# Corner scores of the next heads placed behind the corner of the value sums, ScalarE's other work held back around the sigmoids, and three buffers for v

## The chip, the cores and the metric

The kernel runs on one core of one Trainium2 chip. The metric is the device time of one execution in microseconds (us). Engines: TensorE (PE), VectorE (DVE), ScalarE (ACT), GpSimd (POOL), and SyncE (SP), whose queue issues nearly all DMAs.

## The reference

For 4 batches of 12 heads with 448 positions and head size 64, sigmoid attention; its output goes through a channel mix and then a mixer with a Fourier transform and a feed-forward network:

```python
scores = scale * np.matmul(q, k.transpose(0, 1, 3, 2)) - np.log(S)
attn = 1.0 / (1.0 + np.exp(-scores))
x = np.matmul(attn, v)                      # heads side by side: 768 columns
xk = mu_k * x + (1.0 - mu_k) * x_prev       # x_prev: the position before
k = np.maximum(xk @ w_k, 0.0)
v = k * k @ w_v
r = 1.0 / (1.0 + np.exp(-(xr @ w_r)))       # xr: the same mix with mu_r
# then real(fft2(r*v)) added, a norm, two matmuls with w_ch1 and w_ch2, a sum
```

All is kept near float32: where a product runs in the faster fp32r form, each operand is split into a high and a low part, and three products (high-high, high-low, low-high) are summed.

## The kernel before

The change lies in the first stage, which computes attention and, between its pieces, the keys (`xk @ w_k`). A *pair* is two heads on the 128 partitions: 24 pairs, numbered 0 to 23, six per batch. Pairs go in rounds of two; "round 8" is pairs 8 and 9. A round issues on TensorE, in `attention()`, `both()` and `attnv()`:

- `attnv(i-2)`: the value sums of the two pairs of the round before: first the *corner* of both (tiles `av` from `sg_c`, the last 64 positions), then the rest (`av_6`, `av_7`: 24 matmuls from `sg` and `v`). `join` then copies each sum from PSUM to SBUF on ScalarE (`x<-av`), which frees its PSUM tile, stores `x`, and mixes it (`mix_k`, `xkh`, `xkl`).
- `corner(i)`: the corner scores of the two new pairs (`sc_c`), each head's last 64 positions, from the raw `k` and `q`.
- `scores(i)`, later `scores(i+1)`: six score tiles each (`sc`). `weigh` turns each tile into weights with a sigmoid on ScalarE (`sg<-sc`). Pairs 0 to 5 use float32 matmuls, later ones three fp32r products of split `k` and `q`; the split is a cast on ScalarE (`kh`, `qh`) and a subtraction on VectorE (`kl`, `ql`).

Score tiles, corner tiles and (from pair 6 on) the sums `av` share six PSUM tiles, taken in turn (`slot`). A round takes 2 for `av`, 2 for the corner, 6 and 6 for the scores. So scores 3 and 4 of a round's first pair take over the tiles of its two `av`, once `x<-av` has read them.

Between these pieces TensorE gets the matmuls of the keys (`k`, 18 for each of 8 tiles of a batch). Their results use two further PSUM tiles in turn (`bank`). `key_done` has ScalarE apply relu (`kt<-k`, which frees the tile) and square, then cast to the high part (`kp<-kt`); VectorE subtracts, and SP's queue stores both parts (`k2_d<-kp`). `kp` has two buffers, so the cast of a key tile waits until the store of the tile two before has landed. `k`, `q` have two raw buffers each, `v` two.

The order of every queue is set while the program is built: the class `Order` walks generators in a modelled time, and each engine's instructions stand in the order in which the generators emit them. Its model has costs of engines and DMAs and no PSUM or SBUF tile that is still taken; on the chip each engine works in the emitted order and waits on semaphores. `PACES` are due times in a round for the second scores and for the next round; `o.feed` holds key matmuls that fill the gaps; `weights()` splits the weights for the keys and later stages on VectorE (`LATER`: when it begins, `EVERY`: its pace).

Of the kernel before, what the change touches and what calls it, by code (L numbers as in the profile page):

```python
# [12 lines left out]
F32 = mybir.dt.float32  # L13
F32R = mybir.dt.float32r
# [6 lines left out]
B, H, S, DH = 4, 12, 448, 64  # L21
# [9 lines left out]
PACES = (12.6, 19.6)  # L31
BEGIN = 3
HELD = 4
LATER = 8.0
EVERY = (9.6, 8.5)

SL = np.r_[np.arange(2, 129, 2), np.arange(1, 128, 2)]
LL = np.r_[0, np.arange(130, 255, 2), np.arange(129, 256, 2)]
# [79 lines left out]
class Order:  # L118
# [9 lines left out]
    def __init__(self, nc):  # L128
        self.nc = nc
        self.now = 0.0  # L130
        self.free = {}
        self.heap = []
        self.count = 0
        self.hold = False
        self.rate = 340e3
        self.feed = deque()
        self.at = {}
# [17 lines left out]
    def others(self):  # L155

        self.hold = True
        yield self.now

    def run(self, until=None):  # L160

# [95 lines left out]
def build(tc, ap):  # L257
    nc = tc.nc
    V, G = nc.vector, nc.gpsimd
    o = Order(nc)  # L260
# [7 lines left out]
    def shift(pl, name, n=1):  # L268
        pl.tile([128, int(16 * n)], F32, tag=f"shift_{name}", name=f"shift_{name}", bufs=1)
# [83 lines left out]
    att = pool(s_r, "att", 2, "right")  # L353
# [5 lines left out]
    wkh = wkp.tile([128, NF, KD, 128], F32R, name="wkh")  # L359
    wkl = wkp.tile([128, NF, KD, 128], F32R, name="wkl")  # L360

    pair_t, raw_t, sg_t, xk_t = {}, {}, {}, {}
    pairs = [(b, p) for b in range(B) for p in range(NP)]
    WHOLE = NP

    def prepare(what):

        def room_for(i):
            if what == "v":
                return ("av", i - 2) if i > 1 else None  # L370
            if i < WHOLE:
                return ("pair", i - 4) if i > 3 else None
            return ("pair", 2 * i - 10) if i < WHOLE + 2 else (what, i - 2)

        for i, (b, p) in enumerate(pairs):
            if room_for(i):
                yield from o.issued(room_for(i))
            if what != "v" and i > WHOLE + 1:
                yield from o.issued(("corner", (i - 2) // 2 * 2))
            shape = {"k": [128, 4, 128], "q": [128, S], "v": [128, 4, 2, DH]}[what]  # L380
            odd = what != "v" and i < WHOLE and i % 2
            if what == "q" and i == 1:
                shift(att, "qh")
            raw = att.tile(shape, F32, tag=what + "h" if odd else what, name=f"{what}_{i}", bufs=2)
            if i == 0 and what == "k":
                o.dma(raw[:, 0], ap[what][b, p, :, 0])
                t = o.dma(raw[:, 1:4], ap[what][b, p, :, 1:4])
            else:
                if i == 0 and what == "v":
                    nc.scalar.activation(raw[:, 0, 0, 0:1], bias_s, AF.Sigmoid)  # L390
                t = o.dma(raw, ap[what][b, p], nc.scalar if what == "q" and i < 2 else None)
            if what == "v" or i < WHOLE:
                pair_t[what, i] = raw_t[what, i] = raw
                o.at[what, i] = o.at["raw", what, i] = t
                yield o.now if i == 0 and what != "v" else t
            else:
                raw_t[what, i] = raw
                o.at["raw", what, i] = t
                yield t
                yield from o.issued(("pair", 2 * i - 9 if i < WHOLE + 2 else i - 2))  # L400
                if i == WHOLE:
                    shift(att, "att" + what, 1 + (what == "k"))
                hi, lo = (att.tile(shape, F32R, tag=what + x, name=f"{what}{x}_{i}", bufs=2) for x in "hl")
                pair_t[what, i] = hi, lo
                yield o.act(hi, raw)
                o.at[what, i] = t = o.sub(V, lo, raw, hi)
                yield t

    places = [(c, j) for c in range(3) for j in range(2)]
    half = [slice(0, 64), slice(64, 128)]
# [28 lines left out]
    def corner(i):  # L441
        yield from o.need(*(("raw", w, i + m) for m in range(2) for w in "kq"))
        ps = [slot(f"sc_{i}_c{j}") for j in range(2)]
        for j in range(2):
            for m in range(2):
                k, q = raw_t["k", i + m], raw_t["q", i + m]
                o.mm(ps[j][half[m], 0:S], k[half[j], 3, 64 * j : 64 * j + 64], q[half[j]], True, True, 0.21)
        o.at["corner", i] = o.now
        yield from o.others()
        for j in range(2):  # L450
            weigh(i, f"c{j}", ps[j])
        yield from o.others()

    def both(i, t0):
        if i > 0:
            yield from corner(i)
        yield from o.need(("k", i), ("q", i))
        yield from scores(i)
        if i == 0:
            yield from corner(i)  # L460
        o.at["pair", i] = o.now
        if i > WHOLE + 1:
            yield t0 + PACES[0] * (len(o.feed) > 0)
        yield from o.need(("k", i + 1), ("q", i + 1))
        yield from scores(i + 1)
        o.at["pair", i + 1] = o.now

    def attnv(i):
        ps = [(bank if i < WHOLE else slot)(f"av_{i + m}") for m in range(2)]
        yield from o.need(("sg", i, "c0"), ("sg", i, "c1"))  # L470
        for m in range(2):
            v = pair_t["v", i + m]
            for j in range(2):
                o.mm(ps[m][half[j], 0:S], v[half[m], 3, j], sg_t[i, f"c{j}"][half[m]], True, False, 0.21, skip=True)
        yield from o.others()
        for m in range(2):
            v = pair_t["v", i + m]
            for n, (c, j) in enumerate(places):
                yield from o.need(("sg", i + m, n))
                sg = sg_t.pop((i + m, n))  # L480
                o.mm(ps[m][half[j], 0:S], v[:, c, j], sg, False, c == 2, 0.39, skip=True)
                yield from o.others()
            o.at["av", i + m] = o.now
            o.spawn(join(i + m, ps[m]), o.now + 0.2)

    def join(i, ps):
        if i > 1:
            yield from o.issued(("mixed", i - 2))
        x = att.tile([128, S + 1], F32, tag="x", name=f"x_{i}")
        G.memset(x[:, 0:1], 0.0)  # L490
        yield o.act(x[:, 1 : S + 1], ps[:, 0:S])
        b, p = pairs[i]
        o.dma(x_d[b][p], x)
        if b > 1:
            yield from o.issued(("key", b - 2))
        xh = mop.tile([128, S], F32R, tag=f"xkh{p}", name=f"xkh_{i}")
        xl = mop.tile([128, S], F32R, tag=f"xkl{p}", name=f"xkl_{i}")
        xk_t[b, p] = (xh, xl)
        yield from mix(x, mu_k, att, p, f"k{i}", xh, xl, ("xk", b, p))
        o.at["mixed", i] = o.now  # L500

    def mix(x, mu, pl, p, nm, xh, xl, key, bufs=2):
        xk = pl.tile([128, S], F32, tag="mix", name=f"mix_{nm}", bufs=bufs)
        early = nm[0] == "k" and int(nm[1:]) < WHOLE
        if early:
            yield o.ts(xk, x[:, 1 : S + 1], mu[:, 0, p : p + 1], None, ALU.mult, ALU.bypass)
        else:
            yield o.act(xk, x[:, 1 : S + 1], AF.Copy, scale=mu[:, 0, p : p + 1])
        yield o.stt(xk, x[:, 0:S], mu[:, 1, p : p + 1], xk, ALU.mult, ALU.add)
        if early:  # L510
            V.tensor_copy(xh, xk)
            yield o.spend(V, 0.34)
        else:
            yield o.act(xh, xk)
        o.at[key] = t = o.sub(V, xl, xk, xh)
        yield t
# [6 lines left out]
    def attention():  # L523
        for i in range(0, len(pairs) + 2, 2):
            t0 = o.now
            if i > 0:
                yield from o.need(("v", i - 2), ("v", i - 1))
                yield from attnv(i - 2)
            if i < len(pairs):
                yield from both(i, t0)  # L530
            yield t0 + PACES[1] * (len(o.feed) > 0)
        yield from o.need(("xk", B - 1, NP - 1))
        o.at["attention"] = o.now

    def key_done(b, f, ps):
        t = mop.tile([128, S], F32, tag="kt", name=f"kt_{b}_{f}")
        o.act(t, ps, AF.Relu)
        yield o.act(t, t, AF.Square)
        parts = mop.tile([128, 2, S], F32R, tag="kp", name=f"kp_{b}_{f}")
        yield o.act(parts[:, 0], t)  # L540
        yield o.sub(V, parts[:, 1], t, parts[:, 0])
        o.at["k2_d", b, f] = o.dma(k2_d[b][f], parts.bitcast(F32)) + 2.0
        yield o.now
# [21 lines left out]
    for f in range(NF + KD):  # L565
        if f < NF:
            src, hl, key = ap["w_k"][f], [w[:, f].rearrange(flat) for w in (wkh, wkl)], ("wk", f)
# [195 lines left out]
    for i, n in enumerate((113, 112, 112, 111)):  # L763
        c = fp.tile([128, 2, TW], F32R, name=f"ct{i}")
# [862 lines left out]
```

## Time and profile before

| | us |
|---|---|
| Median of 3 runs (lowest, highest) | 1166.37 (1165.54, 1166.45) |
| The profiled execution: its own time | 1166.35 |
| Its span, first to last instruction | 1164.5 |
| PE busy in the span | 1155.5 (99%) |
| ACT busy in the span | 572.6 (49%) |
| Attention and keys, on PE's timeline | 3.9 to 263.9 |

The profile is one execution. Matmuls overlap in it: each runs into the next, and one that waits for a tile is shown as long, not as late. So "busy" on PE includes some waiting, and the distance from one start to the next tells more than the share.

### The profile page before, as it was taken

To read this page: it belongs to the slowest core of one execution; us is meant where nothing else is said; L and a number is where in the kernel's file an instruction comes from. 1 tells how busy PE (TensorE), PEld (TensorE's weight loads), DVE (VectorE), ACT (ScalarE), POOL (GpSimd) and SP (SyncE) were. 2 spreads that over 40 slices of the span, in tenths; PEclk is the share of its full clock that TensorE was granted. 3 is DMA by queue.
4 is the path that set the end of the run, shared out by engine and by line. 5 is a ranking of instruction groups with operands and counts; after the bars stand their busy time and mean duration, and the time that the engine had idled before them with its cause. 6 is when DMAs were issued, how large, how long until landed. Compare 5 with 4: busy or idle time off the path is not lost.

```text
span 1164.5 us, 16614 instructions
## 1 busy us (share of the span) xinstructions
PE 1155.5 (99%) x6094; PEld 1011.3 (87%) x6094; DVE 836.5 (72%) x1381; ACT 572.6 (49%) x1051; POOL 96.4 (8%) x138
## 2 busy tenths in 40 slices
PE   8999999999999999999999999999999999999998
PEld 3666667699999999999999999999999999999998
DVE  4777776655743688899988888786567777777762
ACT  6878787765630132243333333333237566665740
POOL 0000000000000000000000000000003143342420
PEclk9999999999999999999999999999999999999999
DMA  6667688868949456377565656654827696978894
GB/s 242 226 207 250 219 313 337 304 243 267 325 152 293 158 175 213 121 276 288 183 236 187 223 197 205 219 191 179 312 95 158 145 197 103 188 132 179 173 200 162
DMA packets 93926, 246.67 MB, mean 212 GB/s; under 512 B 10706, under 2 KB 46612, under 8 KB 93716
## 3 DMA queue, kind: packets, MB, share of 16 engines
q1 hardware_dynamic: 77764, 217.29, 53.0%
q0 software_dynamic: 15792, 27.86, 15.1%
q8 instruction: 48, 0.79, 0.3%
q10 hardware_dynamic: 288, 0.46, 0.1%
q14 instruction: 34, 0.28, 0.1%
HBM read 147.02 MB, written 100.61 MB: 213 GB/s over the span
## 4 chain that ended last, share of the span: by engine, by line
PE 97%; ACT 1%; DMA 1%; issue 0%; SPq 0%; DVE 0%
PE f L189 32%; PE m L189 11%; PE v L189 10%; PE k L189 10%; PE r L189 7%; PE av L189 6%; PE f_W L189 4%; PE sc L189 4%; PE f_X L189 4%; PE f_Z L189 4%; PE f_Y L189 2%; PE pq L189 1%; PE sc_c L189 1%; PE pa L189 1%; PE qa L189 1%; DMA v<-in_v 1%
## 5 line engine op out<-in xcount | busy, mean ns | idle before, releaser
L189 PE MATMUL f<-un,w1h 128*128 128x448 f32 x576 | 164.0, 364 | 0.0
L189 PE MATMUL f<-h,w2h 128*128 128x448 f32 x576 | 163.2, 363 | 0.0
L248 POOL DMA_DIRECT2D u_d<-stage x75 | 64.9, 938 | 603.1 <-DMA m_d<-stage 531.7
L189 PEld LDWEIGHTS f<-un,w1h 128*128 128x128 f32 x576 | 108.1, 188 | 7.5 <-issue 0.6
L189 PEld LDWEIGHTS f<-h,w2h 128*128 128x128 f32 x576 | 108.2, 188 | 7.0
L224 DVE TENSOR_TENSOR acc<-acc,f 128x448 f32<-128x448 f32 x126 | 76.3, 618 | 50.1 <-PE f L189 49.3
L189 PE MATMUL v<-k,wvh 128*128 128x448 f32 x384 | 111.9, 365 | 0.0
L189 PE MATMUL f<-un,w1l 128*128 128x448 f32 x288 | 103.9, 361 | 0.0
L189 PE MATMUL f<-h,w2l 128*128 128x448 f32 x288 | 103.7, 360 | 0.0
L189 PE MATMUL m<-hs,sw_h 128*128 128x448 f32 x324 | 91.4, 363 | 0.0
L243 ACT ACTIVATE sg<-sc,bias_s 128x448 f32<-128x448 f32 x144 | 79.0, 663 | 4.3 <-PE sc L189 4.3
L232 DVE SCALAR_TENSOR_TENSOR w_bits<-w_raw,w_bits 128x768 uint32<-128x768 uint32 x80 | 76.5, 956 | 1.7
L189 PEld LDWEIGHTS v<-k,wvh 128*128 128x128 f32 x384 | 72.0, 188 | 4.9 <-issue 0.6
L243 ACT ACTIVATE h<-f 128x448 fp32r<-128x448 f32 x48 | 26.2, 546 | 92.7 <-PE f L189 92.7
L189 PE MATMUL k<-xkh,wkh 128*128 128x448 f32 x192 | 70.7, 368 | 0.0
L189 PE MATMUL k<-xkl,wkh 128*128 128x448 f32 x192 | 70.4, 367 | 0.0
L189 PE MATMUL k<-xkh,wkl 128*128 128x448 f32 x192 | 70.0, 365 | 0.0
L189 PE MATMUL v<-k,wvl 128*128 128x448 f32 x192 | 69.7, 363 | 0.0
L189 PEld LDWEIGHTS m<-hs,sw_h 128*128 128x128 f32 x324 | 60.8, 188 | 4.0
L241 ACT COPY stage<-m 128x448 f32<-128x448 f32 x105 | 55.9, 536 | 15.9 <-DMA u_d<-stage 10.4
L189 PE MATMUL m<-hs,sw_l 128*128 128x448 f32 x162 | 58.4, 360 | 0.0
L189 PEld LDWEIGHTS f<-un,w1l 128*128 128x128 f32 x288 | 53.9, 187 | 3.9 <-issue 0.2
(230 smaller groups left out, 2520.2 us busy)
## 6 DMA issues: line engine op xcount, KB each, us to landing
w_raw<-in_w SPq DMA_DIRECT2D x40, 768.0 KB, 4.8
u_d<-stage POOLq DMA_DIRECT2D x75, 224.0 KB, 5.9
w_d<-w_bits SPq DMA_DIRECT2D x40, 384.0 KB, 2.6
k_d<-kp SPq DMA_DIRECT2D x32, 448.0 KB, 4.1
k<-k_d SPq DMA_DIRECT2D x32, 448.0 KB, 6.0
a<-w_d SPq DMA_DIRECT2D x24, 384.0 KB, 5.7
w<-w_d SPq DMA_DIRECT2D x24, 384.0 KB, 10.8
v<-in_v SPq DMA_DIRECT2D x24, 256.0 KB, 3.6
```

What stands on the lines that cost most here:

```text
L189: self.nc.tensor.matmul(out, lhs, rhs, start=start, stop=stop, skip_group_check=skip)
L224: eng.tensor_tensor(out, a, c, op=op)
L232: self.nc.vector.scalar_tensor_tensor(out, a, scalar, c, op0=op0, op1=op1)
L241: self.nc.scalar.copy(out, a)
L243: self.nc.scalar.activation(out, a, fn, **kw)
L248: self.nc.gpsimd.dma_start(out, src, accum_op=ALU.add)
```

## The change

The corner scores of the next two pairs move from behind the value sums to directly behind the corner of the value sums (except rounds 2 and 6, `BEHIND`). In round 2 the second pair's sums come between its two blocks of scores (`TURNS`). `v` gets three buffers. While a round's scores are due or running, `calm()` holds back new work for ScalarE: casts of `k` and `q`, mixes, squares and casts of keys; `soon()` sets that flag, `begin()` and `both()` clear it. Splits of `k` and `q` become generators of their own (`divide`). The weights begin at 13.5 in place of 8.0 and go at 9.0 in place of 9.6.

```diff
-LATER = 8.0
-EVERY = (9.6, 8.5)
+LATER = 13.5
+AHEAD = 1.0
+NV = 3
+TURNS = (2,)
+BEHIND = (2, 6)
+EVERY = (9.0, 8.5)
...
+    def calm(self):
+
+        while self.quiet:
+            yield self.now + 0.1
...
-                return ("av", i - 2) if i > 1 else None
+                return ("av", i - NV) if i >= NV else None
...
-                yield from o.issued(("corner", (i - 2) // 2 * 2))
+                yield from o.issued(("corner", (i - 2) // 2 * 2), (what, i - 2))
...
+    def divide(what, i, raw, shape):
+        yield from o.issued(("pair", 2 * i - 9 if i < WHOLE + 2 else i - 2))
+        if i > WHOLE:
+            yield from o.issued((what, i - 1))
+        yield from o.calm()
...
+        yield o.act(hi, raw)
+        o.at[what, i] = t = o.sub(V, lo, raw, hi)
+        yield t
...
+    def soon(*keys):
+        o.quiet = all(k in o.at for k in keys)
+
+    def both(i, t0, turn=None):
+        if i in BEHIND:
             yield from corner(i)
...
-        if i > WHOLE + 1:
+        o.quiet = o.quiet and i < WHOLE
+        if turn:
+            yield from turn
+        if i >= WHOLE:
+            yield t0 + (PACES[0] - AHEAD) * (len(o.feed) > 0)
+            soon(("k", i + 1), ("q", i + 1))
             yield t0 + PACES[0] * (len(o.feed) > 0)
...
+        o.quiet = False
+
+    def begin(i):
         ps = [(bank if i < WHOLE else slot)(f"av_{i + m}") for m in range(2)]
         yield from o.need(("sg", i, "c0"), ("sg", i, "c1"))
+        o.quiet = False
...
+    def attnv(i):
+        v = pair_t["v", i]
+        for n, (c, j) in enumerate(places):
...
+            if i % 2 and n == 2 and i < len(pairs) - 2 and i + 1 not in TURNS:
+                g = i + 1
+                soon(("k", g), ("q", g))
...
                 yield from o.need(("v", i - 2), ("v", i - 1))
+                yield from begin(i - 2)
+                if i < len(pairs) and i not in BEHIND:
+                    yield from corner(i)
                 yield from attnv(i - 2)
+                turn = attnv(i - 1)
+                if i not in TURNS:
+                    yield from turn
+                    turn = None
             if i < len(pairs):
-                yield from both(i, t0)
+                yield from both(i, t0, turn)
```

`calm()` is also called ahead of the mixes on ScalarE in `mix`, and of the square and the cast in `key_done`. After the stage the orders agree but for single rows that change places.

What this makes of the orders, at three places. TensorE at the start of round 8, before: the last of `av_7`, the corner of pairs 8 and 9, their first scores.

```order
L189 MATMUL av_7_823<-sg_7_4_737,v_7_650 64x448
L189 MATMUL av_7_823<-sg_7_5_739,v_7_650 64x448
L189 MATMUL sc_8_c0_863<-q_8_701,k_8_652 64x448
L189 MATMUL sc_8_c0_863<-q_9_801,k_9_795 64x448
L189 MATMUL sc_8_c1_864<-q_8_701,k_8_652 64x448
L189 MATMUL sc_8_c1_864<-q_9_801,k_9_795 64x448
L189 MATMUL sc_8_0_881<-qh_8_772,kh_8_746 128x448
```

TensorE at the same place in the changed kernel.

```order
L199 MATMUL av_6_764<-sg_6_c0_646,v_6_511 64x448
L199 MATMUL av_6_764<-sg_6_c1_648,v_6_511 64x448
L199 MATMUL av_7_765<-sg_6_c0_646,v_7_604 64x448
L199 MATMUL av_7_765<-sg_6_c1_648,v_7_604 64x448
L199 MATMUL sc_8_c0_777<-q_8_640,k_8_638 64x448
L199 MATMUL sc_8_c0_777<-q_9_660,k_9_658 64x448
L199 MATMUL sc_8_c1_778<-q_8_640,k_8_638 64x448
L199 MATMUL sc_8_c1_778<-q_9_660,k_9_658 64x448
L199 MATMUL av_6_764<-sg_6_0_663,v_6_511 64x448
```

The corner scores now stand between the corner and the rest of the value sums, and the scores follow the sums directly.

ScalarE at the start of round 14, before: `x_12`, `x_13` are the copies of the value sums, `kt` and `kp` belong to keys, `sg_14` are sigmoids.

```order
L241 COPY x_12_1502<-av_12_1476 128x448
L243 ACTIVATE mix_k12_1513<-x_12_1502,mu_k_243 128x448
L241 COPY x_13_1520<-av_13_1477 128x448
L243 ACTIVATE kt_1_0_1527<-k_1_0_1404 128x448
L243 ACTIVATE kt_1_0_1527<-kt_1_0_1527 128x448
L243 ACTIVATE mix_k13_1534<-x_13_1520,mu_k_243 128x448
L241 CAST kh_15_1536<-k_15_1489 128x512
L241 CAST qh_15_1545<-q_15_1492 128x448
L241 CAST xkh_12_1511<-mix_k12_1513 128x448
L241 CAST kp_1_0_1555<-kt_1_0_1527 128x448
L243 ACTIVATE sg_14_c0_1560<-sc_14_c0_1548,bias_s_241 128x448
```

ScalarE at the same place in the changed kernel.

```order
L253 ACTIVATE kt_0_7_1457<-kt_0_7_1457 128x448
L251 CAST kp_0_6_1461<-kt_0_6_1381 128x448
L253 ACTIVATE sg_14_c0_1493<-sc_14_c0_1482,bias_s_241 128x448
L253 ACTIVATE sg_14_c1_1495<-sc_14_c1_1483,bias_s_241 128x448
L251 CAST kp_0_7_1503<-kt_0_7_1457 128x448
L251 COPY x_12_1516<-av_12_1473 128x448
L251 COPY x_13_1546<-av_13_1474 128x448
L253 ACTIVATE sg_14_0_1549<-sc_14_0_1536,bias_s_241 128x448
```

Mixes and casts of `k` and `q` have left the place between the copies and the sigmoids; the cast `kp_0_7` now stands ahead of the copies. It writes the buffer that the store of `kp_0_5` reads.

SP's queue in round 14 of the changed kernel: raw `k` and `q` of the pairs to come, then that store.

```order
L260 DMA wr_2_raw_1447<-in_w_r 128x1536
L260 DMA k_16_1488<-in_k 128x512
L260 DMA q_16_1490<-in_q 128x448
L260 DMA k_17_1498<-in_k 128x512
L260 DMA q_17_1500<-in_q 128x448
L260 DMA k2_d0_5_88<-kp_0_5_1409 128x896
```

In the kernel before, `k2_d0_5` follows a weight load (`wr_0_raw`) that is not tied to a corner; now it follows four loads, the first of which waits until the corner scores of pair 14 have been computed, since they read the buffer.

## Rows read from the trace of the kernel before

**Rows 1.** Page, part 1: engine, busy us, share of the span, instructions.
```profile
PE 1155.5 (99%) x6094; PEld 1011.3 (87%) x6094; DVE 836.5 (72%) x1381; ACT 572.6 (49%) x1051; POOL 96.4 (8%) x138
```

**Rows 2.** Windows: stretch, then PE, PEld, DVE, ACT, POOL busy us (instructions), clock, DMA.
```profile
160.00:180.00 20.00, 20.00 (x121) 13.56 (x119) 9.19 (x15) 15.89 (x30) 0.20 (x2) 1.00 0.83 313
```

**Rows 3.** Chain that ended last: start us, us, work; pieces that run without a wait.
```profile
9.47 2.46 PE sc L189 x12
...
70.94 2.01 PE sc L189 x18
72.96 5.21 PE k L189 x25
...
83.74 0.91 PE sc_c L189 x8
84.65 2.16 PE sc L189 x18
```

**Rows 4.** The same chain: pieces of scores that take longer.
```profile
18.41 5.45 PE sc L189 x23
...
30.34 4.39 PE sc L189 x19
34.76 1.54 PE sc L189 x4
...
43.59 2.15 PE sc L189 x18
...
48.89 8.80 PE k L189 x43
```

**Rows 5.** Timeline of PE: start us, us, instruction [idle before]; heads 10 to 19.
```profile
113.60 0.97 PE L189 MATMUL av<-sg_c,v 64*64 64x448 f32 x4 [0.30 <-ACT sg L243]
...
115.75 4.73 PE L189 MATMUL av<-sg,v 128*64 128x448 f32 x24
...
123.34 0.47 PE L189 MATMUL sc<-qh,kh 64*128 64x448 f32 x2
...
126.86 0.48 PE L189 MATMUL k<-xkh,wkh 128*128 128x448 f32 x1
...
195.46 0.47 PE L189 MATMUL sc<-qh,kh 64*128 64x448 f32 x2
...
198.22 0.47 PE L189 MATMUL k<-xkh,wkl 128*128 128x448 f32 x1
```

**Rows 6.** Timeline of ScalarE (ACT) in one round: start us, us, instruction.
```profile
67.36 0.70 ACT L243 ACTIVATE mix_k<-x,mu_k 128x448 f32<-128x448 f32 x1
67.92 0.59 ACT L241 CAST xkh<-mix_k 128x448 fp32r<-128x448 f32 x1
...
71.96 3.26 ACT L243 ACTIVATE sg<-sc,bias_s 128x448 f32<-128x448 f32 x6
...
75.08 0.60 ACT L241 CAST kp<-kt 128x448 fp32r<-128x448 f32 x1
75.53 0.59 ACT L243 ACTIVATE kt<-k 128x448 f32<-128x448 f32 x1
76.15 0.58 ACT L243 ACTIVATE kt<-kt 128x448 f32<-128x448 f32 x1
76.64 0.60 ACT L241 CAST kh<-k 128x512 fp32r<-128x512 f32 x1
77.15 0.56 ACT L241 CAST qh<-q 128x448 fp32r<-128x448 f32 x1
```

**Rows 7.** Timeline of SP's queue: two loads issued behind each other.
```profile
64.27 0.33 SPq L250 DMA_DIRECT2D k<-in_k  x1
64.66 0.43 SPq L250 DMA_DIRECT2D q<-in_q  x1
```

**Rows 8.** Waits of SP's queue, 40 to 264 us: us in total, times, longest.
```profile
SPq L250 <- PE sc_c L189: 7.0, 6, 2.2
```

**Rows 9.** Tile k_d (a key part's store), 50 to 264 us: issue to landing.
```profile
DMA to landing us min/median/max: 2.4/4.2/7.3
```

More of the change, by code (lines that the diff above doesn't have):

```diff
@@ L134, in __init__ @@
         self.hold = False
+        self.quiet = False
         self.rate = 340e3
@@ L360, in build @@
     wkl = wkp.tile([128, NF, KD, 128], F32R, name="wkl")
-    pair_t, raw_t, sg_t, xk_t = {}, {}, {}, {}
+    pair_t, raw_t, sg_t, xk_t, av_t = {}, {}, {}, {}, {}
     pairs = [(b, p) for b in range(B) for p in range(NP)]
@@ L383, in prepare @@
                 shift(att, "qh")
-            raw = att.tile(shape, F32, tag=what + "h" if odd else what, name=f"{what}_{i}", bufs=2)
+            raw = att.tile(shape, F32, tag=what + "h" if odd else what, name=f"{what}_{i}", bufs=NV if what == "v" else 2)
             if i == 0 and what == "k":
@@ L394, in prepare @@
                 o.at[what, i] = o.at["raw", what, i] = t
-                yield o.now if i == 0 and what != "v" else t
+                yield o.now if (i == 0 and what != "v") or (i > NV and what == "v") else t
             else:
@@ L398, in prepare @@
                 o.at["raw", what, i] = t
[L399 to L407, printed above, removed]
+                o.spawn(divide(what, i, raw, shape), t)
+                yield o.now + 0.2
+    def divide(what, i, raw, shape):
[3 more added lines that the diff above has]
+        yield from o.calm()
+        if i == WHOLE:
+            shift(att, "att" + what, 1 + (what == "k"))
+        hi, lo = (att.tile(shape, F32R, tag=what + x, name=f"{what}{x}_{i}", bufs=2) for x in "hl")
+        pair_t[what, i] = hi, lo
+        yield o.act(hi, raw)
+        o.at[what, i] = t = o.sub(V, lo, raw, hi)
+        yield t
     places = [(c, j) for c in range(3) for j in range(2)]
@@ L452, in corner @@
         yield from o.others()
-    def both(i, t0):
-        if i > 0:
+    def soon(*keys):
+        o.quiet = all(k in o.at for k in keys)
+    def both(i, t0, turn=None):
+        if i in BEHIND:
             yield from corner(i)
@@ L466, in both @@
         o.at["pair", i + 1] = o.now
-    def attnv(i):
+        o.quiet = False
+    def begin(i):
         ps = [(bank if i < WHOLE else slot)(f"av_{i + m}") for m in range(2)]
         yield from o.need(("sg", i, "c0"), ("sg", i, "c1"))
+        o.quiet = False
         for m in range(2):
@@ L475, in attnv @@
         yield from o.others()
[L476 to L484, printed above, removed]
+        av_t[i], av_t[i + 1] = ps
+    def attnv(i):
+        v = pair_t["v", i]
+        for n, (c, j) in enumerate(places):
+            yield from o.need(("sg", i, n))
+            sg = sg_t.pop((i, n))
+            o.mm(av_t[i][half[j], 0:S], v[:, c, j], sg, False, c == 2, 0.39, skip=True)
+            if i % 2 and n == 2 and i < len(pairs) - 2 and i + 1 not in TURNS:
+                g = i + 1
+                soon(("k", g), ("q", g))
+            yield from o.others()
+        o.at["av", i] = o.now
+        o.spawn(join(i, av_t.pop(i)), o.now + 0.2)
+        yield from o.others()
     def join(i, ps):
@@ L507, in mix @@
         else:
+            yield from o.calm()
             yield o.act(xk, x[:, 1 : S + 1], AF.Copy, scale=mu[:, 0, p : p + 1])
@@ L513, in mix @@
         else:
+            yield from o.calm()
             yield o.act(xh, xk)
@@ L525, in attention @@
             t0 = o.now
+            turn = None
             if i > 0:
                 yield from o.need(("v", i - 2), ("v", i - 1))
+                yield from begin(i - 2)
+                if i < len(pairs) and i not in BEHIND:
+                    yield from corner(i)
                 yield from attnv(i - 2)
+                turn = attnv(i - 1)
+                if i not in TURNS:
+                    yield from turn
+                    turn = None
             if i < len(pairs):
-                yield from both(i, t0)
+                yield from both(i, t0, turn)
             yield t0 + PACES[1] * (len(o.feed) > 0)
@@ L537, in key_done @@
         o.act(t, ps, AF.Relu)
+        yield from o.calm()
         yield o.act(t, t, AF.Square)
         parts = mop.tile([128, 2, S], F32R, tag="kp", name=f"kp_{b}_{f}")
+        yield from o.calm()
         yield o.act(parts[:, 0], t)
```

## Prediction

> **What bounds the kernel now.** Read the shares of the engines first: PE is busy 99% of the span [rows 1], so at first sight there is nothing to gain without taking matmuls away, and this change takes none. The windows say where to doubt it. From 160 to 180 us PE is "busy" for 20.00 of 20.00, its weight loads for 13.56 and ScalarE for 15.89 [rows 2]: a matmul that waits for a PSUM tile is drawn long, so waits hide inside PE's busy time. So take the chain of work that ended last, which lies on PE nearly throughout, and compare like pieces. Undisturbed, six float32 score tiles take 2.46 us, six fp32r tiles 2.01 (2.16 as a round's first), 25 key matmuls 5.21, the corner 0.91 [rows 3]. What is longer is a wait.
>
> **The waits that the change can take away.**
> - Scores 2 and 3 take 5.45 us [rows 4]; two blocks of 2.46, less one switch of kind (0.2, below), are 4.7: **0.7**. The value sums of pair 1 now stand between them.
> - Scores 4 and 5 start at 30.34 and end at 36.30 (34.76 + 1.54) [rows 4]: 5.96, so **1.2**. Their corner and the casts of `k`, `q` leave ScalarE's queue between these sigmoids.
> - Scores 6 and 7 take 43.59 to 48.89 [rows 4], 5.3 against two blocks of 2.01 less a switch, 3.8: **1.5**. 12 key matmuls now lie between them.
> - In round 12's sums PE is idle 0.30, and the corner runs from 113.60 to 115.75, 2.15 against 0.91 [rows 3, 5]: **1.5**, a load of `v` that came late. A third buffer lets it be issued one pair of sums earlier, with about a round to land; if that cover were gone, these 1.5 us come back.
> - Scores 14 run from 123.34 to 126.86 [rows 5], 3.5 against 2.16: **1.4**. ScalarE had mixes and casts ahead of the corner's sigmoids; these sigmoids now fall under the value sums.
> - Scores 21 take from 195.46 to 198.22 [rows 5], 2.76 against 2.01: **0.75**, and scores 23 as much. One key matmul stood between the two blocks; now 22 do, in both rounds.
>
> Sum: 0.7 + 1.2 + 1.5 + 1.5 + 1.4 + 1.5 = **7.8 us**.
>
> **Switches of kind.** 18 more key matmuls cost 8.80 - 5.21 = 3.59 [rows 3, 4], 0.20 each, so 25 of them cost 5.0 and the piece has 0.2 more: the price of going from one kind of matmul to another. Counting along PE's order up to the receptance, there are 79 such places before and 77 now, but nine of the 77 lie between the two corners, which have the same 64 x 64 shape. If those are free, 11 x 0.2 = **2.2 us** go; if they cost as much as the rest, 0.4. I take them as free, since within one kind matmuls follow at 0.20. The Trainium skill (TensorEngine Tiling (Array Packing), Key Properties) says that a change of tiling mode drains TensorE, and a change of tile within a mode doesn't. By that rule the saving is 2.2, without it 0.4; no row of before shows the two corners side by side.
>
> So 10.0 us can go. No instruction is added.
>
> **What takes their place.** Let S be the start of a round's first scores.
>
> *Small ones.* Scores 5 end one sigmoid behind (0.15), and in round 8 the corner waits for two tiles of scores 7, whose sigmoids have just begun (0.3): **0.45**, estimates from the pace of the sigmoids, 3.12 us for six [rows 6].
>
> *Key tiles.* Two PSUM tiles serve the keys, and the relu that frees one stands in ScalarE's queue behind sigmoids and casts. A typical round: sigmoids from S+0.9 to 4.0, then mix, `kh`, mix, `qh` at 0.56, 0.51, 0.56, 0.46 to 6.1, relu 0.62 and square 0.49 to 7.2 [rows 6]. The second scores start at S+6.8 (2.16 + 22 key matmuls 4.6), their sigmoids run 7.7 to 10.8, then `kh`, `qh`, `xkh`, `kp`, `xkh` (0.45 each for the last three) to 13.1, and the next relu ends at 13.7. PE wants that tile in round 8 after 8.8 + 20 matmuls, at 12.9, and in round 18 after 19, at 12.7: waits of 0.8 and 1.0. In round 12 it wants one at 6.3 that is freed at 6.7 (0.4), in round 14 the relu is 0.2 late, which the next item covers. Together **2.3**, lower bound 0; each us that ScalarE runs later adds up to 3.
>
> *The key store behind the loads.* In rounds 10, 14, 16 and 20 a `kp` cast stands ahead of both `x` copies, and it waits for the landing of the store two key tiles back. That store is issued on SP behind loads of `k` and `q` that wait for the corner. SP does wait for corners already, six times, 2.2 us at most [rows 8]. Let A be the start of the value sums. The corner scores end at A+1.7; SP issues at 0.39 apart [rows 7], so `k`, `q`, store at 1.8, 2.2, 2.6 (round 14 has four loads ahead: 3.4). A store takes 2.4 to 7.3 us to land, 4.2 in the median [rows 9]. I take 4.2, the same transfer in the same stage: landed at A+6.8. Then `kp` 0.45, one copy 0.45, the other 0.6 (as the casts of that size [rows 6]): A+8.3. PE ends the sums at A+1.7+4.7 [rows 5], S = A+6.4, and its third and fourth score tiles, 0.7 later, are those of the two sums: wanted at A+7.1. So 1.2 us in three rounds, 2.0 in round 14: **5.6**. With 2.4 it is 0.2 in all, with 7.3 it is 18. Behind the cast wait the copies, the sigmoids, and on VectorE the `kp` subtraction with the weight work behind it; VectorE is busy 9.19 of 20 [rows 2], which absorbs it.
>
> *Priced at nothing.* The weights begin later, but in VectorE's order the first split still stands two rounds ahead of the first key matmul; were one late, PE would stop in full. Casts of `k`, `q` now come a round ahead of their scores. The earlier corner gives the next loads more time, not less.
>
> **Sum.** -7.8 - 2.2 + 0.45 + 2.3 + 5.6 = -1.65 on the profiled execution's 1166.35 us, which is within 0.02 of the median: **1164.7 us**. The rest of the program is unchanged and PE-bound, so a gain here should arrive at the end. About 0.2% (2.3 us) is what can be told from no change.
>
> **Rivals.**
> *The store lands in time.* With landings near 2.4 the waits behind it shrink to 0.2, and the sum is -10.0 + 0.45 + 2.3 + 0.2: **1159.3**. For it: no store of before made a cast wait long enough to appear, and `k`, `q` are small loads. Against it: the median is 4.2, and other loads share the engines.
> *The store decides, and it is slower.* Place: the `kp` cast ahead of the `x` copies in four rounds. It turns the sign once the four waits eat 9.5 us, that is 2.2 each and 3.0 in round 14, landings of 5.2. At 6.0 they cost 3 x 3.0 + 3.8 = 12.8, **1171.9**. For it: 6.0 lies within 2.4 to 7.3, and the loads ahead move over 480 KB first. Against it: it must hold in all four. The Trainium skill (TensorE: Matmul & The Clock Gate, Architectural detail) says that ScalarE's queue is strictly first in, first out. By that, copies that are ready can't pass the waiting cast, and the sum stays; could they pass, it would be the first rival's 1159.3. No row of before shows such a case.
>
> That ScalarE "is kept free" is thus only half true of the order: it is free of mixes, not of that cast.
>
> **Chances.** Forecast 0.45 (own range 1163 to 1168; of it 0.10 faster, 0.33 same, 0.02 slower), store in time 0.35, store decides 0.20. So faster 0.45, same 0.33, slower 0.22. The range leaves out the ends of both rivals: 1158.0 to 1171.5.
>
> **What would show it.** Right: scores 2 to 7, 21 and 23 at 2.0 to 2.5 us a block, no wait for `v`; rounds 10, 14, 16, 20 with first scores of 3 to 4 us, ScalarE idle ahead of `kp` until a store lands; key pieces of rounds 8 and 18 with a hole of about 1 us. Wrong: first scores at 2.2 in those rounds (first rival), at 5 or more (second), or a wait that is none of these, on VectorE or a load.

## The result, and the profile after

The changed kernel takes 1174.65 us (median, 1173.18 to 1174.85) where the kernel before takes 1166.28 beside it: a ratio of 1.0072, 95% interval 1.0061 to 1.0082, so 8.4 us slower. The receptance, the stage behind the keys, starts 8.4 us later on TensorE's timeline, and from there to the end the two traces are the same length: all of the difference lies in attention and keys.

The page after, part 1. PE is as "busy" as in [rows 1]; the shares say nothing here either.

```profile
PE 1155.5 (99%) x6094; PEld 1013.3 (86%) x6094; DVE 834.9 (71%) x1381; ACT 572.5 (49%) x1051; POOL 96.5 (8%) x138
```

PE's timeline after (start us, us, instruction, idle before): scores 2 to 5, and three places further on.

```profile
16.13 2.53 PE L199 MATMUL sc<-q,k 64*128 64x448 f32 x12
...
20.99 2.53 PE L199 MATMUL sc<-q,k 64*128 64x448 f32 x12
23.45 0.98 PE L199 MATMUL av<-sg_c,v 64*64 64x448 f32 x8
24.25 0.93 PE L199 MATMUL sc_c<-q,k 64*64 64x448 f32 x8
25.11 4.73 PE L199 MATMUL av<-sg,v 128*64 128x448 f32 x24
29.77 5.38 PE L199 MATMUL sc<-q,k 64*128 64x448 f32 x24
...
118.35 0.48 PE L199 MATMUL sc<-qh,kh 64*128 64x448 f32 x2
...
122.80 0.90 PE L199 MATMUL sc<-qh,kh 64*128 64x448 f32 x2 [2.97 <-ACT x L251]
...
124.41 0.57 PE L199 MATMUL k<-xkl,wkh 128*128 128x448 f32 x1
...
128.34 0.36 PE L199 MATMUL k<-xkl,wkh 128*128 128x448 f32 x1
...
181.76 0.47 PE L199 MATMUL k<-xkh,wkh 128*128 128x448 f32 x1 [3.58 <-ACT kt L253]
...
193.96 0.91 PE L199 MATMUL sc<-qh,kh 64*128 64x448 f32 x2 [1.41 <-ACT x L251]
```

The first rows are what was hoped for: scores 2 and 3 in two blocks of 2.5 where one of 5.45 stood [rows 4], scores 4 and 5 in 5.3 where it was 5.96, and the two corners side by side. The rest is new. In round 14 (118.35) the first scores stop for 3 us, in round 18 (181.76) a key piece for 3.6, in round 20 (193.96) the scores for 1.4. And behind the hole of round 14 key matmuls follow at 0.37 us instead of 0.20, for ten of them; they are drawn 0.57 us long instead of 0.36. These waits are drawn as idle time of PE, in brackets; part of a wait is still drawn as long matmuls (round 10 loses 1.0 us, of which 0.29 are drawn as idle).

The windows of the changed kernel (as [rows 2]; the number before the last two is the granted clock) show why: in the first of them PE waits, in the other three, each of which begins within 2.1 us of the end of a hole, the clock is at half.

```profile
119.50:122.50 3.00, 0.33 (x4) 0.00 (x0) 0.16 (x1) 0.76 (x2) 0.00 (x0) 1.00 0.56 222
...
124.20:127.40 3.20, 3.20 (x9) 2.80 (x10) 3.10 (x5) 3.20 (x8) 0.00 (x0) 0.51 1.00 258
...
182.50:185.40 2.90, 2.90 (x12) 1.30 (x15) 2.87 (x6) 0.00 (x0) 0.00 (x0) 0.50 0.67 271
...
196.00:199.50 3.50, 3.50 (x11) 3.14 (x10) 1.06 (x2) 3.50 (x8) 0.00 (x0) 0.52 1.03 346
```

0.5 is TensorE's lower level, 1.2 GHz, and PE was idle ahead of each of the three. The chain prices it: 22 key matmuls in rounds 10, 14, 16 and 20; behind the waits of rounds 10 and 16 (1.0 and 1.1 us) there is none.

```profile
79.34 4.62 PE k L199 x22
...
124.11 6.20 PE k L199 x22
...
147.39 4.61 PE k L199 x22
...
195.27 6.20 PE k L199 x22
```

6.20 - 4.62 = 1.6 us for a slow stretch; in round 18 it falls on the last key matmuls and the two corners and costs 1.6 as well.

**Round 14, the wait.** ScalarE's timeline: the cast `kp` at 121.75 waited 5.36 us for its store, and both copies `x` follow it.

```profile
114.78 0.55 ACT L251 CAST kp<-kt 128x448 fp32r<-128x448 f32 x1
115.23 1.15 ACT L253 ACTIVATE sg_c<-sc_c,bias_s 128x448 f32<-128x448 f32 x2
121.75 0.56 ACT L251 CAST kp<-kt 128x448 fp32r<-128x448 f32 x1 [5.36 <-DMA k_d<-kp]
122.22 0.96 ACT L251 COPY x<-av 128x448 f32<-128x448 f32 x2
```

SP's timeline: that store is issued at 115.70, behind four loads, of which the first waited for the corner scores, which end at 113.8.

```profile
113.86 0.33 SPq L260 DMA_DIRECT2D k<-in_k  x1
114.28 0.38 SPq L260 DMA_DIRECT2D q<-in_q  x1
114.76 0.37 SPq L260 DMA_DIRECT2D k<-in_k  x1
115.22 0.38 SPq L260 DMA_DIRECT2D q<-in_q  x1
115.70 0.38 SPq L260 DMA_DIRECT2D k_d<-kp  x1
...
171.19 0.32 SPq L260 DMA_DIRECT2D w_d<-first_w_bits  x1
```

It takes 6.0 us to land, until about 121.7. In the rounds 10, 16 and 20 the store follows two loads, and takes 4.2, 4.3 and 5.3 us to land. (The chain names a load of `v`, 116.21 and 6.03 us, as what released the copies of round 14. But the copies follow the cast at 0.47 us there as in the other three rounds, and the first experiment, which moves the key store alone, takes the wait away.) Over the stage, tile `k_d`:

```profile
DMA to landing us min/median/max: 2.5/4.6/10.3
```

**Round 18, the wait.** VectorE's timeline: a step of the weight split waits 6.4 us for the store of the weights before it, which SP issued only at 171.19 (above), though its data were ready at 164.0. Behind it stand the mixes, the splits of `k` and `q` and, at 185.25, the subtraction `kp`. The step ahead of it, at 170.51, had waited 4.91 us for a load of weights: from 163.8 to 183.8 VectorE works 8.59 us, and nearly all of the rest is these two waits.

```profile
164.05 0.56 DVE L322 CAST w<-first_w_bits 128x768 fp32r<-128x768 f32 x1
...
177.44 0.56 DVE L246 TENSOR_SCALAR first_w_bits<-first_w_raw 128x768 uint32<-128x768 uint32 x1 [6.36 <-DMA w_d<-first_w_bits]
177.92 0.68 DVE L242 SCALAR_TENSOR_TENSOR mix_k<-x,mu_k,mix_k 128x448 f32<-128x448 f32 x1
...
185.25 0.62 DVE L234 TENSOR_TENSOR kp<-kt,kp 128x448 fp32r<-128x448 f32 x1
```

ScalarE's casts wait for these mixes, the relu behind them is late, and PE's key tile with it. The kernel before had the same wait (5.6 us, up to 179.4) at a place where nothing that TensorE wanted stood behind it:

```profile
179.41 0.56 DVE L236 TENSOR_SCALAR first_w_bits<-first_w_raw 128x768 uint32<-128x768 uint32 x1 [5.58 <-DMA w_d<-first_w_bits]
```

### The profile page after: what moved, and what is told of

Read it like the earlier page. It is cut to its first block, busy times and chain, and to the rows that moved or that the text cites. A ratio compares the mean times of both kernels' runs of the same rounds, so it can differ in the third digit from the quotient of the medians.

```text
span 1173.0 us, 16623 instructions
## 1 busy us (share of the span) xinstructions
PE 1155.5 (99%) x6094; PEld 1013.3 (86%) x6094; DVE 834.9 (71%) x1381; ACT 572.5 (49%) x1051; POOL 96.5 (8%) x138
## 4 chain that ended last, share of the span: by engine, by line
PE 94%; DMA 3%; ACT 2%; DVE 1%; issue 1%; SPq 0%; DVEq 0%; ACTq 0%
PE f L199 32%; PE m L199 11%; PE v L199 10%; PE k L199 8%; PE r L199 7%; PE av L199 4%; PE sc L199 4%; PE f_W L199 4%; PE f_X L199 4%; PE f_Z L199 4%; PE f_Y L199 2%; PE pq L199 1%; DMA k<-in_k 1%; PE pa L199 1%; PE qa L199 1%; ACT sg L253 1%
## 5 line engine op out<-in xcount | busy, mean ns | idle before, releaser
L199 PE MATMUL f<-un,w1h 128*128 128x448 f32 x576 | 164.0, 364 | 0.0
```

The costliest lines, as they stand in the source:

```text
L199: self.nc.tensor.matmul(out, lhs, rhs, start=start, stop=stop, skip_group_check=skip)
```

## The experiments

Ratios are against the kernel before, run beside each. The first four test, one by one, that TensorE waits for the two kinds of stores, and that the early corner is what put them late.

### Key stores on another queue

```diff
-        o.at["k2_d", b, f] = o.dma(k2_d[b][f], parts.bitcast(F32)) + 2.0
+        o.at["k2_d", b, f] = o.dma(k2_d[b][f], parts.bitcast(F32), nc.gpsimd) + 2.0
```

> The changed kernel, with only the stores of the key parts (k_d<-kp) issued on GpSimd's queue instead of SP's; the orders of TensorE, VectorE and ScalarE stay as they are. Theory A (the store stands on SP behind loads that wait for the corner, the cast kp waits for its landing, the copies x stand behind the cast, and the slow clock follows these holes): the first scores of rounds 10, 14, 16 and 20, now 3.01, 5.69, 3.11 and 4.13 us, fall to 2.0 to 2.2, which is 7.9 us, and the slow stretches behind those of rounds 14 and 20 go, 1.6 us each: 1174.65 - 11.1 = 1163.6. Rival B (the store lands late because the DMA engines are full, whatever the queue): the first scores stay at 3 to 5 us and the time within 3 us of 1174.65.

Measured: 1167.64 us (1163.8 to 1168.81), ratio 1.0011 [1.0001, 1.0021]; 7 us of the 8.4 are gone. The first scores of rounds 10, 14 and 16 take 2.0 to 2.1 us and the clock stays up behind them: A holds there, B falls there. Waits of scores for a copy `x` (us in total, times, longest), in the changed kernel and in this run:

```profile
PE sc L199 <- ACT x L251: 5.1, 4, 3.0
PE sc L199 <- ACT x L251: 4.1, 1, 4.1
```

The one left is round 20, which takes 7.0 us in the profiled execution, with a slow stretch behind; its chain:

```profile
177.40 7.83 DMA k_d<-kp
...
186.37 1.47 PE sc L199 x6
```

The store starts as soon as its data are there, but the subtraction that makes them stood behind round 18's wait on VectorE, and then it took 7.83 us to land, so for this round B is not refuted. Round 18's key piece, which the edit wasn't meant for, falls from 9.77 to 6.62 us: the weight store, still on SP, now goes out 2 us behind its data instead of 7. The 7 us gained are therefore not A's alone: the trace has 7.4 less in rounds 10, 14 and 16, with their slow stretch, about 4 less in round 18, and 2.7 more in round 20. A cast that waits for a store, ahead of copies that TensorE needs, stays dangerous on any queue.

### Weight stores on another queue

```diff
-                o.dma(w_d[nm][2 * g + i], w)
+                o.dma(w_d[nm][2 * g + i], w, nc.gpsimd)
```

> The changed kernel, with only the stores of the weights that come last in the stage (w_d<-first_w_bits and its neighbour) issued on GpSimd's queue; everything else as it is. Theory C (in round 18 VectorE's weight step waits 6.4 us for this store, issued on SP at 171.2 us though its data were there at 164; behind it the mixes, the key subtraction, a relu, and TensorE's key tile wait): the key piece of round 18, now 9.77 us, falls to 5.2 to 6.2 and the slow clock behind it goes, 1.6 us: 1174.65 - 5 = 1169.5. Rival (the load of the DMA engines sets the landing, or another wait takes its place): 1173 to 1175.

Measured: 1171.83 us, ratio 1.0046 [1.0029, 1.0062]. The key piece of round 18 takes 6.44 us, 1.2 more than undisturbed, at full clock: C holds, though 6.44 lies a little above its 5.2 to 6.2, and 1.2 is near the 1.0 that the prediction had for that tile. The gain is 2.8 instead of 5, as round 20's first scores now take 5.1 us in place of 4.1.

### Both

The two edits together.

> The changed kernel with both kinds of stores on GpSimd's queue. If theories A and C hold and their places are apart: 1174.65 - 11.1 - 5 = 1158.5, below the kernel before (1166.28), with about 2 us of waits for key tiles left in rounds 8, 12 and 14. If the holes only hide one another: above 1163.

Measured: 1162.35 us (1159.63 to 1164.95), ratio 0.9970 [0.9958, 0.9982]: 12.3 us faster than the changed kernel, 3.4 faster than before, with TensorE's and ScalarE's orders untouched. The profiled execution took 1159.63; all waits of TensorE that its trace names from 20 to 290 us are the key tiles of rounds 8, 12, 14 and 18:

```profile
PE k L199 <- ACT kt L253: 2.3, 4, 0.9
```

The median is 3.9 us above the expected time. The executions spread over 5 us; the run with the cast behind the copies (below) is narrower.

### The corner back behind the value sums

```diff
-BEHIND = (2, 6)
+BEHIND = tuple(range(2, 24, 2))
```

> The changed kernel with the corner scores of every round behind the value sums again (BEHIND holds all rounds); the third buffer for v, the hold on ScalarE, and the rest stay. The loads of k and q then stand on SP behind the key stores in three of the four rounds. Theory A: the first scores of rounds 10, 14, 16 and 20 fall to 2 to 3 us, and the slow clock behind them goes (-11.1); nine switches of kind come back (+1.8): about 1165.5. Rival D (it is the key cast ahead of the copies and the hold on ScalarE, not the loads; both are still there): within 2 us of 1174.65.

Measured: 1173.78 us, ratio 1.0069 [1.0054, 1.0084]. The time is D's, the places are A's. The first scores of rounds 10, 14 and 20 take 2.15 us, so the holes there go with the loads, and D is wrong about them. Two others came in their place. PE's timeline:

```profile
141.55 0.91 PE L199 MATMUL sc<-qh,kh 64*128 64x448 f32 x2 [1.34 <-ACT x L251]
...
236.81 0.74 PE L199 MATMUL k<-xkh,wkh 128*128 128x448 f32 x1 [4.11 <-ACT kt L253]
```

A piece of the chain ahead of the second:

```profile
225.22 6.18 DMA k_d<-kp
```

Round 16, where a store still follows the loads, and the first keys after the last sums, where the cast again waits for a store (6.18 us) ahead of the copies: with their slow stretches they cost 3.0 + 2.4 and 6.6 us. Round 18's key piece, on the other hand, takes 6.45 us instead of 9.77, although VectorE still waits 5.2 us for the weight store: only the second of the two mixes stands behind that wait here. So the total doesn't tell the theories apart; a count of what went and what came does.

### The cast behind the copies

In `key_done`, the cast waits while a flag is up that `begin` sets and the second pair's copy clears:

```diff
-        yield from o.calm()
+        while o.quiet or o.sums:
+            yield o.now + 0.1
         yield o.act(parts[:, 0], t)
```

> The changed kernel with one thing moved on ScalarE: a cast kp whose turn falls between the corner of the value sums and the copies x now stands behind both copies; TensorE's order is the same, and all stores stay on SP. Theory A (the copies wait because they stand behind a cast that waits for its store): the first scores of rounds 10, 14, 16 and 20 fall to 2.0 to 2.2 us whenever the store lands, and the slow clock behind them goes: 1174.65 - 11.1 = 1163.6, with round 18's hole of 3.7 us still there. Rival E (the later cast makes the key subtraction, its store and the next relu later, so the wait moves into the key pieces): the key pieces of these rounds take 6.5 to 8 us instead of 5.2, and the time is 1168 to 1174.

Measured: 1167.68 us, ratio 1.0012 [1.0002, 1.0022]. The first scores of all four rounds are undisturbed: A holds. Key pieces grow, as E says, but mainly at another place: rounds 18 and 20 have holes of 2.3 and 3.3 us, the second with a slow stretch.

```profile
174.18 0.47 PE L200 MATMUL k<-xkh,wkh 128*128 128x448 f32 x1 [2.30 <-ACT kt L254]
...
195.67 0.48 PE L200 MATMUL k<-xkh,wkh 128*128 128x448 f32 x1 [3.26 <-ACT kt L254]
```

The chain ahead of the second:

```profile
184.78 6.55 DMA w_d<-first_w_bits
```

Ahead of both holes VectorE waits for a weight store, 6.2 and 6.9 us, and in round 20 the key subtraction now stands behind that wait. So they are theory C at work; what E alone gives is seen in the next run, where the weight stores are out of the way: chiefly half a us more in round 12's key piece (5.83 for 5.36).

> As the run before, and both kinds of stores on GpSimd's queue. Theories A and C: no wait of TensorE hangs on a store any more but through the key tiles: 1158.5 to 1160, and the executions, which spread from 1159.6 to 1165.0 with the cast ahead of the copies, spread over less than 2.5 us. Rival E: 1162 or more, with holes in key pieces.

Measured: 1160.72 us, ratio 0.9957 [0.9942, 0.9971], and a spread of 1.7 us (1159.83 to 1161.54; four executions against ten of the run with both stores). What is left are key tiles, 3.2 us.

### Which part of the change is worth what

With both stores on GpSimd's queue, so that the holes don't hide it: in one run the corner back, in another the hold taken away.

```diff
-        while self.quiet:
+        if False:
             yield self.now + 0.1
```

> The changed kernel with both kinds of stores on GpSimd's queue (median 1162.35) and the corner scores of every round behind the value sums again. If the early corner is worth the nine switches of kind alone: +1.8, 1164.2. If it also takes the corner's sigmoids out of the way of the scores: 1166 to 1168. If it does harm through the loads that it releases early even with the stores elsewhere: below 1162.

Measured: 1165.13 us, ratio 0.9994 [0.9982, 1.0006], 2.8 us above the run with both stores (median against median). Between the two readings: its profiled execution (1164.10) also loses 1.8 us at the first keys after the last sums. The early corner is worth something; that it is just its switches is not shown.

> The changed kernel with both kinds of stores on GpSimd's queue (median 1162.35) and the hold on ScalarE's other work taken away, so that mixes and casts stand between the sigmoids again; TensorE's order is the same. If the hold is worth what the prediction counted for rounds 14 and 4 to 5: first scores of 2.5 to 3.5 us in several rounds, 1164 to 1167. If it does nothing once the corner's sigmoids are early: within 1.5 us of 1162.35.

Measured: 1158.68 us, ratio 0.9936 [0.9920, 0.9953], 3.7 us *faster* without the hold. Neither reading: the hold costs. Without it the relu that frees a key tile comes earlier in the queue; the key pieces of rounds 8 and 14, 1.0 and 0.4 us too long with the hold, are undisturbed. What remains are 0.4 us in two key pieces each and 3.0 in the first scores of round 20. The reason is only in part shown: the two profiled executions are alike in time (1159.63, the fastest of ten, and 1160.09, the slowest of four), and no trace shows the slower executions of the kernel with the hold. Nor is the hold what shortened the scores: without it scores 4 and 5 take the same 5.32 us, and round 14's first scores are undisturbed too.

### The hold alone

The same edit on the changed kernel, all stores on SP.

> The changed kernel with the hold on ScalarE taken away and nothing else; all stores stay on SP. Without the hold the key casts are emitted earlier, and on SP the stores k2_d0_5, k2_d1_0 and k2_d1_5 then stand ahead of the loads that wait for the corner. If the hold is what pushed them behind (theory F, a form of A): the first scores of rounds 10, 14, 16 and 20 fall to 2.0 to 2.8 us and their slow clock goes, round 18's hole of 3.7 us and its slow clock stay: 1163 to 1165. If the early corner alone does it: 1171 to 1175.

Measured: 1164.22 us, ratio 0.9983 [0.9973, 0.9992]: 10.4 us come back by taking away one wait of the planner. F holds. SP's timeline in round 14, where the store `k2_d0_5` is now ahead of the loads:

```profile
109.43 0.33 SPq L260 DMA_DIRECT2D k_d<-kp  x1
111.45 0.33 SPq L260 DMA_DIRECT2D k<-in_k  x1
```

All first scores take 2.0 us from round 8 on. Round 18's wait is still there and even longer (VectorE waits 6.29 us for the weight store, PE 5.2):

```profile
PE k L199 <- ACT kt L253: 5.2, 1, 5.2
```

### Holes of set length

On the kernel with both stores and without the hold (1158.68), superfluous copies on ScalarE ahead of the last `x` copy in rounds 10, 16 and 22.

```diff
+LATE_COPIES = {9: 4, 15: 8, 21: 3}
...
+        for n in range(LATE_COPIES.get(i, 0)):
+            nc.scalar.copy(x[:, 1 : S + 1], ps[:, 0:S])
```

> The changed kernel with both kinds of stores on GpSimd's queue and without the hold (median 1158.68), and 4, 8 and 3 superfluous copies of a value sum on ScalarE ahead of the last copy x in rounds 10, 16 and 22. At 0.43 us a copy, first scores that want the tile 0.7 us into their piece wait about 1.4, 3.2 and 1.0 us there. If a hole costs only its length: 1158.7 + 5.6 = 1164.3, and the key matmuls behind it follow at 0.20 us. If the clock falls after a hole: key matmuls at 0.37 us for about 10 of them (1.6 us) behind the long one; the short ones tell whether holes like those of rounds 10 and 16 of the changed kernel (0.85 and 0.95 us, no slow stretch behind) stay free of it: about 1166 with one slow stretch, 1167.5 with two.

Measured: 1167.20 us (1165.85 to 1169.31), 8.5 above its base. PE's timeline around the holes of rounds 10 and 16, and the windows behind them and behind round 22's (about 1 us):

```profile
78.34 0.47 PE L200 MATMUL sc<-qh,kh 64*128 64x448 f32 x1 [1.34 <-ACT x L252]
...
79.66 0.37 PE L200 MATMUL k<-xkl,wkh 128*128 128x448 f32 x1
...
143.31 0.74 PE L200 MATMUL sc<-qh,kh 64*128 64x448 f32 x1 [3.61 <-ACT x L252]
...
145.63 0.57 PE L200 MATMUL k<-xkl,wkh 128*128 128x448 f32 x1
```

```profile
79.00:83.00 4.00, 4.00 (x22) 3.62 (x20) 1.04 (x2) 4.00 (x9) 0.00 (x0) 1.00 0.85 305
...
143.60:148.20 4.60, 4.60 (x14) 3.67 (x13) 1.76 (x4) 4.60 (x10) 0.00 (x0) 0.50 1.03 351
209.50:213.00 3.50, 3.50 (x19) 3.23 (x18) 1.98 (x4) 3.50 (x7) 0.00 (x0) 1.00 1.02 336
```

Behind the hole of 3.61 us the clock is at half, and the 22 keys take 6.3 us, 1.7 more than undisturbed; behind the two shorter ones it stays at full. In the same kernel without the copies the clock stays at full at this place, so the slow stretch comes with the hole. A hole of 1.34 us also stood ahead of the slow stretch of the run with the corner back, and 1.41 in round 20 of the changed kernel: the length of a hole alone doesn't settle it.

### The best version, and the stores on the kernel before

> The changed kernel with both kinds of stores on GpSimd's queue, without the hold, and with the cast kp behind the copies x. The waits left in the run without the hold were 0.35 and 0.37 us in two key pieces and 2.8 us in the first scores of round 18 or 20 (a copy and corner sigmoids behind a cast): if these go, 1156 to 1157.5; if the later cast moves them into key pieces (theory E), 1158 to 1160.

Measured: 1157.38 us (1156.88 to 1157.98), ratio 0.9924 [0.9909, 0.9939]: 17.3 us faster than the changed kernel, 8.9 faster than before. All waits of TensorE that its trace names between 20 and 290 us:

```profile
PE k L200 <- ACT kt L254: 0.8, 2, 0.6
```

> The kernel before, with both kinds of stores on GpSimd's queue. No wait of TensorE hung on them there (the cast kp stood behind the copies): 1165 to 1167, no difference from 1165.8. If stores on SP also cost the kernel before something that its chain does not show: 1160 to 1164.

Measured: 1166.26 us, ratio 0.9998 [0.9989, 1.0007]. The other queue is worth nothing that can be told in the kernel before; in the changed kernel it takes away waits that the change made.

## Why the prediction was wrong

**The gain was right.** Count against undisturbed pieces what the changed kernel waits: first scores of rounds 10, 14, 16 and 20, 1.0 + 3.7 + 1.1 + 2.1 = 7.9; key tiles of rounds 8, 12 and 14, 1.0 + 0.75 + 0.4 = 2.15; round 18's, 3.8; three slow stretches, 4.8. Sum 18.65, on a kernel that is 8.4 slower: without them it would be 10.2 us faster. The prediction had 7.8 + 2.2 = 10.0. That the two agree so closely is in part luck. The count leaves out scores 4 and 5 and the corner of round 8, each still 0.4 too long (0.45 predicted for both), and with them the gain is 11.0; and the kernel before also lost 0.9 us in scores 13, 16 and 18, which the prediction's list lacks. The best version, 8.9 us below the kernel before with 0.8 us of named waits left, shows a gain of this size directly. The switch between the joined corners is free as taken: the two take 1.66 us together (23.45 to 25.11), where twice the 0.91 of a corner between other kinds [rows 3] would be 1.82, and the prediction's price of a switch was 0.2. That agrees with the Trainium skill (TensorEngine Tiling (Array Packing), Key Properties), by which it is a change of tiling mode, and not just of tile, that drains TensorE. The late `v` is gone: the sums of round 12 run without a wait.

**The key store behind the loads: mechanism right, 5.6 us taken, 7.9 measured.** The working hits the places to some tenths in three of the four rounds: in round 14 the store was to be issued 3.4 us after the start of the sums, and was at 3.7. (In round 20 it was at 3.7 for 2.6, as the corners ran at half clock.) What failed is "I take 4.2", a median, for the landing. In rounds 10 and 16 it took 4.2 and 4.3 and the waits were 1.0 and 1.1 (predicted 1.2); in rounds 14 and 20 it took 6.0 and 5.3, and they were 3.7 and 2.1 (2.0 and 1.2). The cost grows one for one with the landing, and nothing gains when it is short, so a median is too low. That copies don't pass a cast that waits is shown by the 5.36 us in ScalarE's timeline. This agrees with the Trainium skill (TensorE: Matmul & The Clock Gate, Architectural detail), which calls ScalarE's queue strictly first in, first out.

**Round 18's key tile: 1.0 taken, 3.8 measured.** Two steps failed. One is "VectorE is busy 9.19 of 20 [rows 2], which absorbs it"; the other puts the weights under "Priced at nothing". VectorE's idle time was not slack but in good part waiting for transfers: of the 10.8 us idle in that window of the kernel before, 5.6 were a wait for a weight store, and in the changed kernel two waits for transfers take 11.3 of 20. Its queue stands still while it waits, whatever else is ready. With the weight store elsewhere the tile cost 1.2: the reckoning of ScalarE's queue was sound, the term for VectorE was missing. The wait of 5.6 us was in the trace before; I had priced the weights by their order alone.

**The clock: 0 taken, 4.8 measured.** No step had it. Every hole was priced at its length, while three of them brought 1.6 us of half clock behind. In the kernel before no row of the stage showed it (1.00 in [rows 2]). The Trainium skill (TensorE: Matmul & The Clock Gate, Part 1: The HAM clock gate) says that the clock has two levels and that an idle TensorE is given the lower. These rows agree, though not every hole was followed by the lower level (last section).

Put together: 2.3 for the landings, 2.8 for round 18 and 4.8 for the clock are the 10 us between -1.65 and +8.4; the other differences cancel (other key tiles 2.15 for 1.3, small ones 0.8 for 0.45, gain 11.0 for 10.0). The rival "the store decides" named a right place and the right sign, but its 1171.9 is near by luck: it put the four waits at 12.8, and they were 7.9. With 7.9 in the prediction's sum the kernel comes out 0.65 us slower, which can't be told from no change; it is round 18 and the clock that make it slower for certain. (That the sign turns at 9.5 us of waits is a slip: the sum is zero at 7.25, and 9.5 is where slower could be told. The key tiles as listed add up to 2.2, not 2.3.) Of the signs that the prediction gave, rounds 10 and 16 (3.0 and 3.1 us) show the forecast, round 14 (5.7) the second rival, and round 18 the last, a wait on VectorE.

**The hold.** The prediction saw that ScalarE is "free of mixes, not of that cast", and beyond a share in the gain of scores 4 and 5 it gave the hold no price. It is the hold that made the order bad: it delays the casts, so that their stores are emitted behind the loads. Taken away alone it gives back 10.4 us. The early corner alone doesn't make the loss, as this run has it; nor does the corner moved back alone take it away (1173.78).

What is not shown: why landings differ (4.2 to 6.0) between rounds with like neighbours; no run changed the traffic alone. Nor why SP came to the weight store of round 18 only at 171.19. A third buffer for `kp` wasn't tried.

## What to carry to other kernels

Before an operation is moved ahead of a copy that TensorE needs, look at what it can wait for: in a queue that works in order, a cast that waits for a store to land holds up everything behind it, and a store issued behind a load that waits holds up the cast. Price such a wait by the slow landings, not by the median, and add for each hole of TensorE of some us the slow stretch that may follow. Idle time of an engine is slack only if the trace shows that it waits for the work in question, and not for a transfer.

## What the runs showed of the hardware that was not expected

- A hole in TensorE's work (2.97, 3.58 and 1.41 us in the changed kernel, 3.61 made on purpose) was followed by a stretch at a granted clock of 0.50 to 0.52, in which key matmuls follow at 0.37 us instead of 0.20, before it returned to 1.00: 1.6 us lost per stretch in the changed kernel. After a hole of 1.34 us in one kernel and of 2.30 in another it stayed at full; after holes of 1.34 and 1.41 in two others it fell.
- Moving stores to GpSimd's queue did not shorten the transfers in any steady way: in the median key stores landed in 4.5 us there for 4.6 on SP in the changed kernel, and with the weight stores moved too in 5.4. What it changed is that they were issued when their data were ready.
